# Blockwise causal attention and a maxout layer on one core: all of the layer's weights loaded ahead of two groups of q and k

## The chip, the core, the metric

The kernel runs on one core of a Trainium2 chip. The metric is device time in microseconds (us) from start to end of the program. An engine is named as the profile names it: PE (TensorE, matmuls), PEld (its weight loads), DVE (VectorE), ACT (ScalarE), POOL (GpSimd), SP (SyncE, which here only issues transfers). Each runs its own list of instructions strictly in the order written, and waits for others by semaphores.

## What is computed

Eight batches of eight heads, 576 tokens, head dimension 64, all float32 in and out. Attention is causal by blocks of 64 tokens; its output is laid out as 4608 tokens by 512 and goes through a two-branch layer.

```python
scores = scale * np.matmul(q, k.transpose(0, 1, 3, 2))
mask = block_i >= block_j                  # blocks of 64
attn = softmax(np.where(mask, scores, -1e9))
x = (attn @ v).transpose(0, 2, 1, 3).reshape(4608, 512)
g = np.maximum(x @ w1, x @ w2)             # 512 x 1024 each
out = g @ w_out                            # 1024 x 512
```

## The kernel before

**Algebra.** max(x w1, x w2) is x w2 + relu(x (w1 - w2)). So the kernel forms D = w1 - w2 (`diff_w`, line 183, four column pieces on DVE), M = w2 w_out (`m_unit`, line 249, on PE, after `bT_unit`, line 238, has transposed w2), and then out = relu(x D) w_out + x M. `h_unit(i, f)` (line 226) is one of eight 128-column pieces of relu(x D) for a span i of 512 tokens: four matmuls of 512 columns and an eviction on DVE (line 231). `y_unit` (line 268) is one 128-token tile of the output: four matmuls with M, eight with w_out.

**Attention.** The 64 heads are 32 pairs, two pairs a group, 16 groups; a batch is two groups. For a group, q and k are loaded in float32 (`load_qk`, line 115, on SP's queue), cast to bfloat16 (`cast`, line 155, mostly on POOL), transposed on PE (`transposes`, line 357) and copied out by DVE and ACT (line 365). `pad_keys` (line 383, POOL) makes a padded copy of some key columns. The scores of a pair go through `tile_0`, `tile_1`, `tile_2` (lines 376 and 394) into one of two PSUM buffers; `exp` (line 400, ACT) empties it, with a small corner exp at line 458; `mask` (line 405, POOL) zeroes four corners. `av` (line 486, PE) multiplies with v, and `x_out` transposes the result into xT on PE (lines 524 and 526, copied at 529 and 530; from group 8 on by DMA). `done_tokens` then says how many tokens the layer may work on. The first two groups (pairs 0 to 3) use finer pieces, `burst_*`.

**Order.** The order is written out by hand up to group 2 and by a loop from group 3 on. Between the attention steps, `fill(n)` issues the next ready units of the list bT, M, h, y: n counts 512-column matmuls (an M matmul counts half, a bT transpose a quarter). In the loop `fill_of(g)` sets how much is filled beside group g: the ready work less `KEEP`, shared over the groups left to the next batch boundary. `av_with(p - LAG, lo)` places av two pairs behind the scores.

**Transfers.** w2, w_out, w1 and v are issued by POOL (lines 180, 189, 177, 159) and share one software queue; q, k and the output are issued by SP. A load of q or k with `gated=True` is held back by a POOL memset of one column of its buffer (line 114): SP can issue it only after POOL has come to that place in its list. v(b, c) is piece c of five of batch b's values.

Before, the last part of the hand order runs thus on POOL: masks of pairs 2 and 3, w1(0), gates of group 2, masks, w1(1), w1(2), masks, w1(3), cast of q of group 2, gates of group 3, cast of k, v of batch 1.

Of the kernel before, what the change touches and what calls it, by code (L numbers as in the profile page):

```python
# [10 lines left out]
AF = mybir.ActivationFunctionType  # L11
# [3 lines left out]
def kernel(  # L15
# [10 lines left out]
    nc = tc.nc  # L26
# [4 lines left out]
    HP = H // 2  # L31
# [75 lines left out]
    def load_qk(g, queues, gated=False):  # L107
        b, u = divmod(g, GPB)
        for nm, src, queue in (("q", q, queues[0]), ("k", k, queues[1])):
            if queue is None or by_dma(nm, g):  # L110
                continue
            raws[nm, g] = t = raw.tile([P, 2, RPP * D], FP32, name=f"{nm}raw")
            if gated:
                nc.gpsimd.memset(t[:, 0, :1], 0.0)
            queue.dma_start(
                out=t[:],
                in_=src[b, 4 * u:4 * u + 4].rearrange(
                    "(s h) (p t) d -> (h p) s (t d)", h=2, t=RPP),
            )
# [4 lines left out]
    def by_dma(nm, g):  # L124
        return g >= T_DMA.get(nm, NG)

    def load_blocks(nm, g):
        b, u = divmod(g, GPB)
        blk_n[nm, g] = n = raw.tile([P, S // BLK, 2, D], BF16, name=f"{nm}b", tag=f"{nm}raw")
        for h in range(2):  # L130
            for s in range(2):
                nc.gpsimd.dma_start(  # L132
                    out=n[h * BLK:(h + 1) * BLK, :, s],
                    in_=(q if nm == "q" else k)[b, 4 * u + 2 * s + h].rearrange(
                        "(j p) d -> p j d", p=BLK),
                )
# [10 lines left out]
    def cast(nm, g, parts):  # L147
        if by_dma(nm, g):
            return
        t = raws[nm, g].rearrange("p s (t d) -> p t s d", d=D)  # L150
        if (nm, g) not in qk_n:
            qk_n[nm, g] = qkn.tile([P, RPP, 2, D], BF16, name=f"{nm}n")
        n = qk_n[nm, g]
        for copy, j0, j1 in parts:
            copy(out=n[:, j0:j1], in_=t[:, j0:j1])  # L155

    def load_v(b, c):
        rows = min(P, S - c * P)
        nc.gpsimd.dma_start(  # L159
            out=vv_r[b % NV][P - rows:, c, :, :D],  # L160
            in_=v[b, :, c * P:c * P + rows, :].rearrange("h p d -> p h d"),
        )
# [12 lines left out]
    def load_w1(j):  # L175
        w1_raw[j] = wraw.tile([P, NDM, WB], FP32, name="w1raw")
        nc.gpsimd.dma_start(out=w1_raw[j][:], in_=w1r[:, :, j * WB:(j + 1) * WB])
# [41 lines left out]
    def h_unit(i, f):  # L219
        if f == 0:  # L220
            g_tiles[i] = g_pool.tile([P, NFF, SPAN], BF16, name="g")
        g = g_tiles[i]
        t0 = i * SPAN
        pt = ps_m.tile([P, SPAN], FP32, name="ps_h", tag="m")
        for c in range(NDM):
            nc.tensor.matmul(  # L226
                pt[:], d_sb[:, c, f * P:(f + 1) * P], xT[:, c, t0:t0 + SPAN],
                start=(c == 0), stop=(c == NDM - 1),
            )
            if c == NDM - 1:  # L230
                nc.vector.tensor_scalar_max(g[:, f], pt[:], 0.0)  # L231
            yield

    def bT_unit(j):
# [89 lines left out]
    def ready():  # L324
        return int(sum(n * cost for n, _, need, cost in current + todo if need <= done_tokens[0]))
# [73 lines left out]
    def exp(p, ps, w, a0):  # L399
        nc.scalar.activation(  # L400
            out=aT_r[p % NA][:, :, a0:a0 + w], in_=ps[:, :, :w], func=AF.Exp, scale=scale,
        )

    def mask(p, a0, eng=None):
        (eng or nc.gpsimd).memset(aT_r[p % NA][BLK:, :, a0:a0 + BLK], 0.0)  # L405
# [27 lines left out]
    def masks_q(p, eng=None):  # L433
        for a in (1024, 1408):
            mask(p, a, eng)
# [3 lines left out]
    def tile_0(p):  # L439
        u = ps_s.tile([P, 2, 512], FP32, name="ps_s", tag="s")  # L440
        scores(p, u, 0, 0, 0, 512)
        return lambda: (exp(p, u, 512, 0), mask(p, 0))

    def tile_1(p):
        u = ps_s.tile([P, 2, 512], FP32, name="ps_s", tag="s")
        scores(p, u, 0, 0, 512, 64)
        scores(p, u, 64, 1, 128, 448)
        return lambda: (exp(p, u, 512, 512), mask(p, 576))

    def tile_2(p):  # L450
        u = ps_s.tile([P, 2, 512], FP32, name="ps_s", tag="s")
        corner_scores(p, u, 320)
        scores(p, u, 0, 2, 256, 320)
        scores(p, u, 384, 3, 448, P)

        def out():
            exp(p, u, 512, 1024)
            nc.scalar.activation(  # L458
                out=aT_r[p % NA][BLK:, :, 1536:AW], in_=u[BLK:, :, 320:320 + BLK],
                func=AF.Exp, scale=scale,  # L460
            )
            mask(p, 1024)
            mask(p, 1344)
        return out

    def region(*tiles):
        for out in tiles:
            out()

    def av(p, ts):  # L470
        b, hp = divmod(p, HP)
# [69 lines left out]
    def fill_of(g):  # L541
        if g == NG - 1:
            return 45
        left = 5 - g if g < 5 else 2 - (g - 5) % 2
        return -(-max(0, ready() - KEEP) // left)


    def pool_work(s):
        g, i = divmod(s, 2)
        if s == 4:  # L550
            load_qk(4, (SP, SP), gated=True)
        elif s == 5:
            load_qk(5, (SP, SP), gated=True)
            cast("q", 4, ((pool, 0, RPP),))
            cast("k", 4, ((pool, 0, RPP),))
        else:
            if i == 1 and g + 3 < NG:
                load_qk(g + 3, (SP, SP), gated=True)
            if i == 1 and g + 2 < NG:
                cast("q", g + 2, ((pool, 0, RPP),))  # L560
                cast("k", g + 2, ((pool, 0, RPP),))
            nb, j = divmod(s + 2, HP)
            if nb < B:
                for c in ((0, 1), (2, 3), (4,), ())[j]:
                    load_v(nb, c)
            for nm in "qk":
                if i == 1 and g + 3 < NG and by_dma(nm, g + 3):
                    load_blocks(nm, g + 3)

    T_AT = {s: [("qk"[s % 2], s // 2 + 1)] for s in range(NPAIR - 2)}  # L570
    T_AT[0] = T_AT[1] = T_AT[2] = T_AT[3] = []
# [51 lines left out]
    masks_p(2)  # L623
    masks_p(3)
    load_w1(0)
    load_qk(2, (SP, SP), gated=True)
    fill(2)
    av(1, [2, 3, 4])
    burst_q1(2)
# [13 lines left out]
    av(2, [2, 3, 4])  # L643
    burst_q3(3)
    masks_q(3)
    load_w1(3)
    cast("q", 2, ((pool, 0, RPP),))
    load_qk(3, (SP, SP), gated=True)
    cast("k", 2, ((pool, 0, RPP),))
    load_v(1, 0)  # L650
    fill(8)
    av(3, [2, 3, 4])
    fill(4)
    x_out(1, 0, NCH, (act, act))
    fill(4)
    transposes("q", 2, (dve, act))()
    transposes("k", 2, (dve, act))()
    pad_keys(4)
    pad_keys(5)
    load_v(1, 1)  # L660
    diff_w(0)
    fill(4)
    region(tile_0(4), tile_1(4))
    load_v(1, 2)
    load_v(1, 3)
    fill(8)
    region(tile_2(4), tile_0(5))
    load_v(1, 4)
    diff_w(1)
    fill(8)  # L670
    region(tile_1(5), tile_2(5))
    diff_w(2)
    cast("q", 3, ((pool, 0, RPP),))
    cast("k", 3, ((pool, 0, RPP),))
    fill(4)
    diff_w(3)
    n = fill_of(GPB)
    fill(n // 2)
    transposes("q", 3, (dve, act))()
    pool_work(4)  # L680
    fill(n // 3)
    transposes("k", 3, (dve, act))()
    pad_keys(6)
    pad_keys(7)
    pool_work(5)
    fill(n - n // 2 - n // 3)

    for g in range(GPB + 1, NG):
        a, b = 2 * g, 2 * g + 1
        old = done_tokens[0]  # L690
        if x_due:
            x_out(x_due.pop())
        n, new = fill_of(g), done_tokens[0]
        region(tile_0(a), tile_1(a))
        lo, hi = max(3, n // 18), n * 2 // 9
        for p, tiles in ((a, lambda: (tile_2(a), tile_0(b))), (b, lambda: (tile_1(b), tile_2(b)))):
            done_tokens[0] = old if p == a and x_by_dma(g - 2) else new
            fill(hi)
            av_with(p - LAG, lo)
            done_tokens[0] = new  # L700
            if p % 2 and x_by_dma(g - 1):
                x_dma(g - 1)
            if p % 2 == 0:
                for nm in "qk":
                    if g + 1 < NG and by_dma(nm, g + 1):
                        transpose_blocks(nm, g + 1)
            copy_out = t_pair(p)
            outs = tiles()
            copy_out()
            region(*outs)  # L710
            if p % 2 and g + 1 < NG:
                pad_keys(p + 1)
                pad_keys(p + 2)
            pool_work(p)
        x_due.append(g - 1)
        fill(n - 2 * (lo + hi))
    for p in range(NPAIR - LAG, NPAIR):
        if x_due:
            x_out(x_due.pop())
        av_with(p, 5)  # L720
        if p % 2 and x_by_dma(p // 2):
            x_dma(p // 2)
        fill(9)
# [42 lines left out]
```

## Time and profile before

| | |
|---|---|
| median of 4 runs | 258.94 us (257.89 to 260.35) |
| profiled execution | 258.81 us, its span 257.0 us |
| granted TensorE clock, mean | 0.997 |
| PE busy | 245.9 us, 96% |
| DVE, ACT, POOL busy | 149.9, 119.5, 122.9 us |
| HBM read, written | 34.60, 9.44 MB |
| w1 pieces, issue to landing (median) | 14.9 us |
| first scores of pair 6 (group 3) | 45.36 us |

The span runs from the first to the last instruction; the program's time is 1.8 us longer. All places below are us from the start of the span. Matmuls are pipelined: the record of a 512-column matmul lasts 0.38, but 36 of them follow each other in 7.77, 0.216 each. In a row of the timeline the bracket says how long the engine stood idle before it and what released it. In the waits a row reads: who waited, for whom, us in total, times, longest. In the DMA answers an issue line gives KB each and us from issue to landing, a queue line packets, MB and the time its packets took as a share of 16 engines; q0 is POOL's software queue, q1 SP's.

### The profile page before, as it was taken

What the parts mean: (1) busy time and instruction counts of PE and PEld (TensorE: products, weight loads), DVE (VectorE), ACT (ScalarE), POOL (GpSimd) and SP (SyncE); (2) the same over time, 40 slices, a digit from 0 to 9 for tenths busy, and PEclk for the clock granted to TensorE, in tenths of its full rate; (3) what the DMA queues carried; (4) which work ended last, traced back from release to release, by engine and by line L of the source; (5) the groups of instructions that cost most, each with busy time, mean ns of one, the idle gap of its engine ahead of it and who ended that gap; (6) DMA issues with size and microseconds to landing.
All of it is one profiled execution on the core that took longest, in us unless ns stands there. A gap on an engine that the chain in (4) does not pass through costs nothing.

```text
span 257.0 us, 6746 instructions
## 1 busy us (share of the span) xinstructions
PE 245.9 (96%) x2768; PEld 132.7 (52%) x2768; DVE 149.9 (58%) x300; ACT 119.5 (47%) x159; POOL 122.9 (48%) x289
## 2 busy tenths in 40 slices
PE   8897998989899999999999999999999999999994
PEld 2465753546455555555555555555545564444443
DVE  4986669656576447645754575457535754753521
ACT  2776394687665555555555546464646400000000
POOL 1984475579868456845685568557331100000000
PEclk9999999999999999999999999999999999999998
DMA  7999999979999999999999999999961312101122
GB/s 250 206 160 246 345 311 73 360 55 220 186 169 214 155 219 145 216 158 211 152 210 158 212 154 205 162 214 160 117 127 60 92 42 82 43 35 49 68 95 83
DMA packets 104383, 41.27 MB, mean 161 GB/s; under 512 B 89248, under 2 KB 93728, under 8 KB 104352
## 3 DMA queue, kind: packets, MB, share of 16 engines
q0 software_dynamic: 65952, 11.87, 59.9%
q1 hardware_dynamic: 37984, 28.32, 46.7%
q10 hardware_dynamic: 416, 0.66, 0.7%
q8 instruction: 21, 0.34, 0.6%
q14 instruction: 10, 0.08, 0.2%
HBM read 34.60 MB, written 9.44 MB: 171 GB/s over the span
## 4 chain that ended last, share of the span: by engine, by line
PE 82%; ACT 6%; DMA 5%; POOL 3%; issue 2%; SPq 0%; DVE 0%; POOLq 0%; ACTq 0%
PE ps_y L268 35%; PE ps_h L226 22%; PE ps_o L486 10%; PE ps_s L376 7%; ACT aT L400 4%; DMA kraw<-in_k_dram 4%; PE ps_w L346 2%; PE ps_qT L357 2%; DMA qraw<-in_q_dram 2%; POOL qn L155 1%; PE ps_y L283 1%; POOL kn L155 1%; ACT kT L365 1%; PE ps_s L411 1%; PE ps_s L394 1%
## 5 line engine op out<-in xcount | busy, mean ns | idle before, releaser
L400 ACT ACTIVATE aT<-ps_s 128x1024 bf16<-128x1024 f32 (+2 forms) x100 | 95.8, 994 | 43.7 <-PE ps_s L376 32.7
L268 PE MATMUL ps_y<-wo_sb,g 128*128 128x512 bf16 x280 | 71.2, 380 | 0.0
L226 PE MATMUL ps_h<-xT,d_sb 128*128 128x512 bf16 x288 | 67.9, 380 | 0.0
L231 DVE TENSOR_SCALAR g<-ps_h 128x512 bf16<-128x512 f32 x72 | 49.6, 690 | 18.4 <-PE ps_h L226 18.3
L405 POOL MEMSET aT<- 64x128 bf16 x128 | 23.1, 201 | 66.0 <-ACT aT L400 65.2
L273 DVE COPY y<-ps_y 128x512 f32<-128x512 f32 x35 | 24.2, 692 | 45.5 <-PE ps_y L268 44.7
L486 PEld LDWEIGHTS <-aT 128*128 128x128 bf16 x960 | 37.4, 98 | 14.0 <-issue 0.5
L226 PEld LDWEIGHTS <-d_sb 128*128 128x128 bf16 x288 | 26.5, 98 | 31.3 <-issue 2.5
L268 PEld LDWEIGHTS <-g 128*128 128x128 bf16 x280 | 24.7, 98 | 30.3 <-issue 5.7
L486 PE MATMUL ps_o<-vv,aT 128*128 128x65 bf16 x960 | 39.8, 194 | 0.0
L268 PE MATMUL ps_y<-m_sb,xT 128*128 128x512 bf16 x140 | 38.4, 380 | 0.0
L159 POOL DMA_DIRECT2D vv<-in_v_dram x40 | 33.9, 854 | 1.0 <-issue 0.5
L376 PE MATMUL ps_s<-qT,kT 64*128 64x128 bf16 (+6 forms) x344 | 31.6, 281 | 2.6 <-ACT aT L458 1.5
L493 DVE TENSOR_TENSOR xp<-ps_o,rec 128x256 bf16<-128x256 f32 (+1 forms) x64 | 31.4, 491 | 2.2
L132 POOL DMA_DIRECT2D kb<-in_k_dram x40 | 29.4, 759 | 0.0
L492 DVE RECIPROCAL rec<-ps_o 128x4 f32<-128x4 f32 (+1 forms) x64 | 12.0, 187 | 23.2 <-PE ps_o L486 22.9
L288 ACT COPY y<-ps_y 128x256 f32<-128x256 f32 (+1 forms) x2 | 0.6, 319 | 49.3 <-PE ps_y L283 49.3
L365 ACT COPY qT<-ps_qT 128x576 bf16<-128x576 bf16 x15 | 9.6, 639 | 26.6 <-PE ps_qT L357 26.6
L155 POOL CAST qn<-qraw 128x1152 bf16<-128x1152 f32 (+1 forms) x15 | 17.3, 1154 | 7.5 <-DMA qraw<-in_q_dram 7.4
L268 PEld LDWEIGHTS <-xT 128*128 128x128 bf16 x140 | 12.8, 98 | 13.5 <-issue 0.5
L376 PEld LDWEIGHTS <-kT 64*128 64x128 bf16 x344 | 11.9, 94 | 14.2 <-issue 9.0
L365 DVE COPY qT<-ps_qT 128x576 bf16<-128x576 bf16 x17 | 12.8, 750 | 0.9 <-PE ps_qT L357 0.9
(58 smaller groups left out, 135.9 us busy)
## 6 DMA issues: line engine op xcount, KB each, us to landing
qraw<-in_q_dram SPq DMA_DIRECT2D x16, 576.0 KB, 4.8
out_dram<-y SPq DMA_DIRECT2D x35, 256.0 KB, 3.9
vv<-in_v_dram POOLq DMA_DIRECT2D x32, 128.0 KB, 5.6
kraw<-in_k_dram SPq DMA_DIRECT2D x5, 576.0 KB, 7.5
kb<-in_k_dram POOLq DMA_DIRECT2D x40, 72.0 KB, 6.2
w1raw<-in_moe_w_dram POOLq DMA_DIRECT2D x4, 512.0 KB, 14.9
xT<-in_moe_w_dram POOLq DMA_DIRECT2D x4, 256.0 KB, 6.9
wo_sb<-in_moe_w_out_dram POOLq DMA_DIRECT2D x2, 512.0 KB, 11.9
```

The lines of the kernel that those rows point to most:

```text
L132: nc.gpsimd.dma_start(out=n[h * BLK:(h + 1) * BLK, :, s], in_=(q if nm == "q" else k)[b, 4 * u + 2 * s + h].rearrange("(j p) d -> p j d", ...
L159: nc.gpsimd.dma_start(out=vv_r[b % NV][P - rows:, c, :, :D], in_=v[b, :, c * P:c * P + rows, :].rearrange("h p d -> p h d"),)
L226: nc.tensor.matmul(pt[:], d_sb[:, c, f * P:(f + 1) * P], xT[:, c, t0:t0 + SPAN], start=(c == 0), stop=(c == NDM - 1),)
L231: nc.vector.tensor_scalar_max(g[:, f], pt[:], 0.0)
L268: nc.tensor.matmul(py[:], lhs, rhs, start=(n == 0), stop=(n == len(terms) - 1),)
L273: nc.vector.tensor_copy(out=y[:], in_=py[:])
L365: (copy or copies[i])(out=t[:, p0 * RPP:p1 * RPP].rearrange("q (p j) -> q p j", j=RPP), in_=pts[i][:, :, p0:p1].rearrange("q j p -> q p j"),)
L376: nc.tensor.matmul(ps[:, hh, col:col + w], kT[r, k0:k0 + P], qT[r, q0:q0 + w], start=True, stop=True,)
L400: nc.scalar.activation(out=aT_r[p % NA][:, :, a0:a0 + w], in_=ps[:, :, :w], func=AF.Exp, scale=scale,)
L405: (eng or nc.gpsimd).memset(aT_r[p % NA][BLK:, :, a0:a0 + BLK], 0.0)
L486: nc.tensor.matmul(po[:, gi, hh, :], a[:, hh, a0:a0 + P], vv[:, c, h0 + 2 * hh, :], start=(mm == 0), stop=(mm == n_mm - 1),)
L493: nc.vector.tensor_mul(xp[:, :, ts[0]:ts[0] + n, p % 2].rearrange("q s t d -> q t s d"), po[:, :, :, :D], rec[:, :n].to_broadcast([P, n, 2 ...
```

## The change

It reorders the hand-written part and the start of the loop; no unit of work is added or taken away.

- Loads: q and k of group 2 are gated after w1(0) to w1(2) and before w1(3), group 3 right after w1(3), instead of after w1(0) and after the cast of q. v of batch 1 follows at once, its pieces 0 and 1 ahead of the casts.
- The last five M units run in one piece (part of `fill(4)`, and `fill(16)`) ahead of the transposes of group 2, which stood among them; three of the four `diff_w` come before these transposes; one h unit stands between q's and k's.
- The first two h units are evicted by ACT (relu) instead of DVE.
- Masks of pairs 4 and 5 come in one piece later on POOL (`masked=False`, `masks(p)`), and group 3's transposes stand among the scores of pair 5. Gates and casts of groups 4 and 5 move with them, out of `pool_work`.
- In the loop, av(6) runs at the end of group 3 and av(7) in the slot of pair 8; pair 9's slot takes `x_out(3)`. `KEEP` is 0 up to group 4.

```diff
             if c == NDM - 1:
-                nc.vector.tensor_scalar_max(g[:, f], pt[:], 0.0)
+                if i == 0 and f < 2:
+                    nc.scalar.activation(out=g[:, f], in_=pt[:], func=AF.Relu)
+                else:
+                    nc.vector.tensor_scalar_max(g[:, f], pt[:], 0.0)
             yield
...
+    def masks(p):
+        for a0 in (0, 576, 1024, 1344):
+            mask(p, a0)
+
-    def region(*tiles):
+    def region(*tiles, masked=True):
         for out in tiles:
-            out()
+            out(masked)
...
-        return -(-max(0, ready() - KEEP) // left)
+        return -(-max(0, ready() - (KEEP if g > GPB + 2 else 0)) // left)
...
     masks_p(3)
     load_w1(0)
-    load_qk(2, (SP, SP), gated=True)
     fill(2)
...
     masks_q(3)
+    load_qk(2, (SP, SP), gated=True)
     load_w1(3)
+    load_qk(3, (SP, SP), gated=True)
+    load_v(1, 0)
+    load_v(1, 1)
     cast("q", 2, ((pool, 0, RPP),))
-    load_qk(3, (SP, SP), gated=True)
+    load_v(1, 2)
     cast("k", 2, ((pool, 0, RPP),))
-    load_v(1, 0)
+    load_v(1, 3)
+    load_v(1, 4)
     fill(8)
     av(3, [2, 3, 4])
     fill(4)
     x_out(1, 0, NCH, (act, act))
     fill(4)
+    diff_w(0)
+    diff_w(1)
+    diff_w(2)
+    fill(16)
     transposes("q", 2, (dve, act))()
+    fill(4)
     transposes("k", 2, (dve, act))()
     pad_keys(4)
     pad_keys(5)
-    load_v(1, 1)
-    diff_w(0)
-    fill(4)
-    region(tile_0(4), tile_1(4))
-    load_v(1, 2)
-    load_v(1, 3)
-    fill(8)
-    region(tile_2(4), tile_0(5))
-    load_v(1, 4)
-    diff_w(1)
-    fill(8)
-    region(tile_1(5), tile_2(5))
-    diff_w(2)
+    diff_w(3)
     cast("q", 3, ((pool, 0, RPP),))
+    load_qk(4, (SP, SP), gated=True)
     cast("k", 3, ((pool, 0, RPP),))
     fill(4)
-    diff_w(3)
-    n = fill_of(GPB)
-    fill(n // 2)
-    transposes("q", 3, (dve, act))()
-    pool_work(4)
-    fill(n // 3)
+    region(tile_0(4), tile_1(4), masked=False)
+    fill(8)
+    region(tile_2(4), tile_0(5), masked=False)
+    masks(4)
+    fill(8)
+    copy_out = transposes("q", 3, (dve, act))
+    outs = tile_1(5), tile_2(5)
+    copy_out()
+    region(*outs, masked=False)
+    fill(4)
     transposes("k", 3, (dve, act))()
     pad_keys(6)
     pad_keys(7)
-    pool_work(5)
-    fill(n - n // 2 - n // 3)
+    masks(5)
+    load_qk(5, (SP, SP), gated=True)
+    cast("q", 4, ((pool, 0, RPP),))
+    cast("k", 4, ((pool, 0, RPP),))
+    fill(4)
...
             fill(hi)
-            av_with(p - LAG, lo)
+            if p == 9:
+                x_out(3)
+                new = done_tokens[0]
+            else:
+                av_with(p - 1 if p == 8 else p - LAG, lo)
...
-        x_due.append(g - 1)
+        if g != GPB + 2:
+            x_due.append(g - 1)
         fill(n - 2 * (lo + hi))
+        if g == GPB + 1:
+            av_with(6, lo)
```

More of the change, by code (lines that the diff above doesn't have):

```diff
@@ L441, in tile_0 @@
         scores(p, u, 0, 0, 0, 512)
-        return lambda: (exp(p, u, 512, 0), mask(p, 0))
+        return lambda masked: (exp(p, u, 512, 0), masked and mask(p, 0))
     def tile_1(p):
@@ L447, in tile_1 @@
         scores(p, u, 64, 1, 128, 448)
-        return lambda: (exp(p, u, 512, 512), mask(p, 576))
+        return lambda masked: (exp(p, u, 512, 512), masked and mask(p, 576))
     def tile_2(p):
@@ L454, in tile_2, with out @@
         scores(p, u, 384, 3, 448, P)
-        def out():
+        def out(masked):
             exp(p, u, 512, 1024)
@@ L461, in out @@
             )
-            mask(p, 1024)
-            mask(p, 1344)
-        return out
-    def region(*tiles):
+            if masked:
+                mask(p, 1024)
+                mask(p, 1344)
+        return out
+    def masks(p):
+        for a0 in (0, 576, 1024, 1344):
+            mask(p, a0)
+    def region(*tiles, masked=True):
         for out in tiles:
-            out()
+            out(masked)
     def av(p, ts):
@@ L544, in fill_of @@
         left = 5 - g if g < 5 else 2 - (g - 5) % 2
-        return -(-max(0, ready() - KEEP) // left)
+        return -(-max(0, ready() - (KEEP if g > GPB + 2 else 0)) // left)
     def pool_work(s):
         g, i = divmod(s, 2)
[L550 to L568, printed above, removed]
+        if i == 1 and g + 3 < NG:
+            load_qk(g + 3, (SP, SP), gated=True)
+        if i == 1 and g + 2 < NG:
+            cast("q", g + 2, ((pool, 0, RPP),))
+            cast("k", g + 2, ((pool, 0, RPP),))
+        nb, j = divmod(s + 2, HP)
+        if nb < B:
+            for c in ((0, 1), (2, 3), (4,), ())[j]:
+                load_v(nb, c)
+        for nm in "qk":
+            if i == 1 and g + 3 < NG and by_dma(nm, g + 3):
+                load_blocks(nm, g + 3)
     T_AT = {s: [("qk"[s % 2], s // 2 + 1)] for s in range(NPAIR - 2)}
```

## The prediction

> **What bounds the kernel now.** I read the page first, then stretches of time, then TensorE's waits, then the DMA answers of the stretch that the change touches. TensorE (PE) is full from 70 us to the end of the matmuls, so the time is PE's fixed work plus the holes in its first 70 us.
>
> ```profile
> PE   8897998989899999999999999999999999999994
> PEclk9999999999999999999999999999999999999998
> ```
>
> The stretches give the holes in us (first number the length, second PE busy; the 1.00 after the engines is the granted clock):
>
> ```profile
> 23.40:45.36 21.96, 18.59 (x234) 11.51 (x235) 14.67 (x23) 11.74 (x20) 12.74 (x26) 1.00 1.27 250
> 45.36:70.00 24.64, 23.07 (x398) 13.59 (x399) 14.32 (x34) 17.53 (x23) 20.04 (x45) 1.00 1.09 204
> 70.00:253.00 183.00, 183.00 (x1825) 95.84 (x1824) 102.74 (x201) 74.51 (x97) 75.21 (x182) 1.00 1.05 140
> ...
> 255.50:256.00 0.50, 0.00 (x0) 0.00 (x0) 0.00 (x0) 0.00 (x0) 0.00 (x0) 0.68 0.00 0
> ```
>
> 21.96 - 18.59 = 3.37 us are idle between 23.40 (last scores of pair 3) and 45.36 (first scores of pair 6), 24.64 - 23.07 = 1.57 up to 70, none after. PE's waits from 20 to 70 us name them:
>
> ```profile
> PE ps_M L249 <- DMA wo_sb<-in_moe_w_out_dram: 1.6, 1, 1.6
> PE ps_s L376 <- ACT aT L458: 1.5, 2, 0.8
> PE ps_qT L357 <- POOL qn L155: 1.0, 1, 1.0
> PE ps_kT L357 <- POOL kn L155: 0.5, 1, 0.5
> ```
>
> The first, third and fourth are landings, or casts behind landings; the second is exponentials that hold a score buffer. The whole prize is 3.37 + 1.57 = 4.9 us: no change of order can make this kernel faster than about 253.9.
>
> How long loads take is in the DMA answers, for single issues: w_out's first half, q and k of group 2 (issued 19.19 and 19.60), q and k of group 3 (27.70 and 28.18):
>
> ```profile
> wo_sb<-in_moe_w_out_dram POOLq DMA_DIRECT2D x1, 512.0 KB, 10.6
> qraw<-in_q_dram SPq DMA_DIRECT2D x1, 576.0 KB, 7.2
> kraw<-in_k_dram SPq DMA_DIRECT2D x1, 576.0 KB, 9.9
> qraw<-in_q_dram SPq DMA_DIRECT2D x1, 576.0 KB, 9.6
> kraw<-in_k_dram SPq DMA_DIRECT2D x1, 576.0 KB, 12.5
> ```
>
> And who shares the engines, in three stretches: 19.6 to 22.4, 23 to 27, 32 to 34 us (packets, MB):
>
> ```profile
> q0 software_dynamic: 1096, 0.55, 145.3%
> ```
>
> ```profile
> q1 hardware_dynamic: 447, 0.99, 72.5%
> q0 software_dynamic: 481, 0.25, 44.6%
> ```
>
> ```profile
> q0 software_dynamic: 121, 0.45, 61.5%
> q1 hardware_dynamic: 122, 0.28, 42.0%
> ```
>
> Until 22.4 nothing of group 2 moves, though q was issued at 19.19. Then q, k take 0.99 of 1.24 MB from w_out (small packets), but against w1 (3.7 KB a packet to their 2.3) they get 0.28 of 0.73. Packet counts are about equal in both: the queues take turns by packet.
>
> **The change, part by part.** Times are of the profiled execution: span 257.0, 258.81 in all, 0.13 below the median of the four runs (258.94).
>
> 1. w_out alone. From 22.4 to 25.03 its queue crept at 0.25 MB / 4 us = 62 KB/us instead of 0.55 / 2.8 = 196. With q, k gone, the 0.14 MB moved from 22.8 to 25.0 take 0.7 us: landing at 23.5 at best, 25.03 at worst. I take 24.0, as a straggling engine rather than the mean lands last: PE waits 0.6 from 23.40 instead of 1.63.
>
> 2. M in one piece. In before, two units, an av, a unit (25.03 to 28.50) are 3.47, x_out 0.41, the next unit 0.98. Units 5 to 8 are 32 matmuls at 1.86/16 = 0.116: 3.7. Sum 8.56, so M ends at 24.0 + 8.56 = 32.6. Its evictions go to ACT, idle then. w_out's second half landed 29.7 before; it is needed at 28.9 now, with less ahead of it: nothing.
>
> 3. q, k of group 2 issued later. Their gates pass POOL's masks, w1(1) and w1(2): after the last mask (23.99 + 0.20) the gate is at 24.23, and by the 0.13 from gate to issue SP starts q at 24.36, k at 24.77. SP has nothing else queued. With q's first bytes 3.2 to 3.6 us after issue they meet w1, not w_out. Bounds for k: 9.9 and 12.5 after issue, 34.7 to 37.3. The w1 neighbourhood is that of group 3, though fewer straggling bytes are ahead: I take 11.6, so 36.4; for q 9.0 (of 7.2 to 9.6), 33.4. From landing to the first transpose before: k landed 29.5, the cast ran 1.14, transposes began 30.84, so 1.32.
> PE stands from 32.6 to 34.7 (33.4 + 1.32): 2.1. Then 0.37 of q transposes and one h unit, 0.97: 36.05. k's transposes start at 36.4 + 1.32 = 37.7: 1.65 more. v(1,2) now sits between the casts (0.89 on POOL), done by 35.6, before k lands: nothing. v(1,0) and v(1,1), 0.89 each, run while POOL waits anyway, and their packets queue behind w1. While POOL waits for k, v(1,3), v(1,4) and the pads stand behind it: v(1,4) is issued near 39.5 instead of 37.79 and at its 8.3 lands near 47.8; its av is not before 49, so that costs nothing, with 1.2 to spare.
>
> 4. diff_w ahead of the q copies. Three at 1.23 on DVE, idle there; free unless w1(2) lands after 34.7 (36.6 before; with q, k out of its way I expect 33). Then DVE, in order, holds qT and all behind it.
>
> 5. Relu on ACT for two h units. A 128x256 cast there is 0.37, a 128x1024 exp 1.02, so about 0.6 each; the second stands before the first exp, and one score tile waits 0.15. DVE is spared 2 x 0.69.
>
> 6. Masks, pads, gates for groups 4 and 5, casts: the same instructions. The 4 masks of pair 4 now follow k's cast of group 3 but are needed at its av, some 10 us later; 4 x 0.20 is nothing.
>
> 7. Groups 3 and 4. The 0.82 wait ahead of group 4 goes: av(6), 0.91, and six more y matmuls, 1.3, now lie in it. In group 4 the slot of pair 9 has x_out instead of an av, so ACT leads. ACT before, in that group:
>
> ```profile
> 59.04 0.64 ACT L365 COPY qT<-ps_qT 128x576 bf16<-128x576 bf16 x1 [1.50 <-PE ps_qT L357]
> 59.58 1.03 ACT L400 ACTIVATE aT<-ps_s 128x1024 bf16<-128x1024 f32 x1
> 60.63 0.27 ACT L458 ACTIVATE aT<-ps_s 64x128 bf16<-64x128 f32 x1
> 60.93 1.02 ACT L400 ACTIVATE aT<-ps_s 128x1024 bf16<-128x1024 f32 x1
> ```
>
> From the end of q's transposes (58.85) ACT needs 3.1 to 61.95, then 0.6 copy, 1.95 for two exps, 0.27: 5.9. PE's work up to the second score tile of group 5 was 65.24 - 0.69 - 58.85 = 5.7; less the av (0.91) and one y (0.22): 4.6. So 1.3 idle, where before had 0.69. Net of both: 1.3 - 1.51 = -0.2; bounds -1.5 (ACT ahead by then) and +0.6.
>
> 8. KEEP and the new fill counts move matmuls between slots and add none; PE is full from 70 us on, which hides it. If a slot starved, its units would be missing from the row at 70.
>
> Sum: 0.6 + 2.1 + 1.65 + 0.15 = 4.5 against 3.37, +1.1; step 7, -0.2; +0.9. The other way round: from k's transposes to pair 6 the rows add to 9.2, so 46.9, where before stood at 45.36 with one h unit (0.87) still to do, 46.23: +0.7, less 0.2, +0.5. I take +0.8: **259.6**.
>
> Two rules weigh on this. The Trainium skill, "DMA: Bandwidth & Descriptors", Latency and other measured facts, gives a hardware queue about 0.6 us to its first byte. The trace disagrees under load (nothing from 19.56 to 22.4). By the rule q, k would start about 2.7 us earlier, k land near 34, and the sum be near 257.
>
> The second speaks against the rival below. The skill's "TensorE: Matmul & The Clock Gate", Part 1, says the clock halves after an idle window of about 3.4 us; no wait here is that long, so by it the clock stays and the sum too. The row above gives 0.68 in 255.50 to 256.00, hence a drop at 255.7, only 2.2 us after the last matmul at 253.44.
>
> **The rivals.**
>
> The clock drops (slower). Waits of 2.1 and 1.65 with 1.3 of work between them are near the 2.2 after which it fell; 1.63, the longest wait of before, left it at 1.00. It decides if the wait for q passes some 2.2. Price: 16 warm-up matmuls took 6.21 at the start where 16 x 0.216 = 3.46 would do, so 2.75 at most; the wait for k hides up to 1.65 of it, leaving 1.1 to 2.75, I say 1.8: 261.4.
>
> The loads come as fast as group 2's did (7.2 and 9.9). For: fewer bytes ahead. Against: w1 in large packets. k at 34.7 takes 1.7 from the waits: 257.9; with ACT's new wait gone too, 256.4.
>
> The queue of group 3 slips: its casts were waited for 0.98 in before, one of them ran 1.96 instead of 1.14, and its loads now follow group 2's at once. Against: it is needed 6 and 8 us after k's transposes. About +2: 261.6.
>
> The reordering is hidden anyway, landings and all: 258.8; it is inside the main case's range.
>
> **How the numbers follow.** Main case 0.48, own range 258.2 to 260.8; fast loads 0.24 (255.8 to 258.2); clock 0.18 (260.8 to 262.6); group 3 late 0.10. What this kernel's measurement can tell is about 1%, 2.6 us: under 256.35 is faster, over 261.53 slower. Faster: half of the fast loads, 0.12. Slower: half of the clock case, 0.09, most of the late one, 0.07, a little of the main, 0.02: 0.18. Same: 0.70. The range leaves out the outer tenth on each side: 256.5 to 261.8.
>
> **What would show it.** PE's wait for w_out near 0.6; q and k of group 2 landing near 33.4 and 36.4; PE waits of about 2 and 1.6 us on the two casts; the first scores of pair 6 near 47; a wait of some 1.3 on the exps in group 4; clock 1.00 throughout. k before 35 or a clock under 1.00 would make it wrong.

## The result and the profile after

| | before | after |
|---|---|---|
| median | 258.93 us (64 runs, 257.37 to 264.98) | 260.05 us (43 runs, 258.94 to 262.06) |
| profiled execution, its span | 258.81, 257.0 | 259.87, 258.1 |
| granted TensorE clock, mean | 0.997 | 0.993 |
| first scores of pair 6 | 46.23 (45.36 and the h unit that came later) | 47.98 |

The ratio of after to before is 1.0047, 95% interval [1.0031, 1.0063]: 0.5% slower, less than the 1% that the prediction held this measurement able to tell, but with an interval that excludes 1. Runs over 1.5% above the fastest of the same kernel are left out of the ratios and of the groups by clock below, not of the medians in the tables; of those timed with the experiments all but one, of 631 us, had a mean clock of 0.985 to 0.993.

The page's first hint is one digit: PE's and the clock's share of the span, in 40 slices.

```profile
PE   8897959999899999999999999999999999999994
PEclk9999988999999999999999999999999999999999
```

The two 8s in the clock, missing before, lie at and behind the 5 in PE: TensorE waited, and then ran slower. The stretches of after, with the same columns as before (length, then PE busy; after the engines, clock):

```profile
23.40:45.36 21.96, 18.01 (x212) 11.29 (x212) 11.71 (x18) 9.93 (x17) 11.99 (x24) 0.92 1.32 278
45.36:70.00 24.64, 23.73 (x371) 13.17 (x367) 14.44 (x33) 19.49 (x27) 17.32 (x44) 1.00 0.97 161
70.00:254.00 184.00, 184.00 (x1879) 97.10 (x1877) 103.96 (x205) 75.57 (x98) 78.72 (x187) 1.00 1.08 142
```

Here 3.95 us are idle in the first stretch (3.37 before) and its clock is 0.92; 0.91 in the second (1.57 before); none later. PE's waits from 20 to 73 us (who, for whom, us, times, longest):

```profile
PE ps_qT L360 <- POOL qn L155: 2.4, 1, 2.4
PE ps_M L252 <- DMA wo_sb<-in_moe_w_out_dram: 1.3, 1, 1.3
PE ps_kT L360 <- POOL kn L155: 0.6, 1, 0.6
PE ps_kT L360 <- DVE xT L537: 0.4, 1, 0.4
PE ps_s L379 <- ACT aT L461: 0.3, 1, 0.3
```

The same in PE's timeline (start, duration, instructions, wait in brackets):

```profile
24.41 1.92 PE L252 MATMUL ps_M<-wo_sb,bT_sb 128*128 128x256 bf16 x16 [1.27 <-DMA wo_sb<-in_moe_w_out_dram]
...
28.29 4.54 PE L252 MATMUL ps_M<-wo_sb,bT_sb 128*128 128x256 bf16 x40
35.21 0.44 PE L360 MATMUL ps_qT<-ident,qn 64*128 64x64 bf16 x18 [2.38 <-POOL qn L155]
35.58 1.04 PE L226 MATMUL ps_h<-xT,d_sb 128*128 128x512 bf16 x4
37.18 0.66 PE L360 MATMUL ps_kT<-ident,kn 64*128 64x64 bf16 x18 [0.56 <-POOL kn L155]
37.77 1.89 PE L226 MATMUL ps_h<-xT,d_sb 128*128 128x512 bf16 x4
```

The same four matmuls of an h unit take 1.04 at 35.58 and 1.89 at 37.77. Where the clock lies, the stretches show:

```profile
33.25:36.67 3.42, 1.41 (x22) 0.63 (x22) 1.15 (x2) 0.65 (x2) 2.66 (x3) 1.00 1.21 338
36.67:40.08 3.41, 2.90 (x28) 1.15 (x28) 1.89 (x2) 1.60 (x3) 3.26 (x5) 0.50 1.97 206
```

In 3.42 us of mostly waiting PE is busy for 1.41; the next 3.41 are at half clock. And the landings, for single issues in stretches that hold only one, q and k of group 2:

```profile
qraw<-in_q_dram SPq DMA_DIRECT2D x1, 576.0 KB, 9.7
kraw<-in_k_dram SPq DMA_DIRECT2D x1, 576.0 KB, 11.1
```

Issued at 24.12 and 24.53, they landed at 33.8 and 35.6. In the rows of POOL the casts follow:

```profile
34.01 1.14 POOL L155 CAST qn<-qraw 128x1152 bf16<-128x1152 f32 x1 [7.18 <-DMA qraw<-in_q_dram]
35.10 0.88 POOL L159 DMA_DIRECT2D vv<-in_v_dram  x1
35.97 1.16 POOL L155 CAST kn<-kraw 128x1152 bf16<-128x1152 f32 x1
```

Who shares the engines, from q's issue to its first bytes (24.12 to 27.9 us), and from there to 34 us (packets, MB, share):

```profile
q0 software_dynamic: 628, 1.33, 114.4%
```

```profile
q1 hardware_dynamic: 529, 1.17, 56.3%
q0 software_dynamic: 526, 0.96, 50.6%
```

Nothing of q moves for 3.8 us. Then the packets are equal in number, as before, and q and k get 1.17 of 2.13 MB.

In group 4, ACT's rows answer to those shown of before:

```profile
63.00 0.64 ACT L368 COPY qT<-ps_qT 128x576 bf16<-128x576 bf16 x1 [1.21 <-PE ps_s L397]
63.54 1.03 ACT L403 ACTIVATE aT<-ps_s 128x1024 bf16<-128x1024 f32 x1
...
66.36 1.95 ACT L403 ACTIVATE aT<-ps_s 128x1024 bf16<-128x1024 f32 x2
68.33 0.27 ACT L461 ACTIVATE aT<-ps_s 64x128 bf16<-64x128 f32 x1
```

From the first copy on ACT has no pause until the corner exp at 68.33, whose end releases PE's scores at 68.66.

The ledger, up to pair 6: the three waits are 1.27 + 2.38 + 0.56 = 4.21, against 3.37 idle before: +0.84. PE came to the first of them 0.25 earlier (23.15 for 23.40). Pair 6 is 47.98 - 46.23 = 1.75 late, so 1.75 - 0.84 + 0.25 = 1.16 are left for the clock. Behind it: 0.44 + 0.33 = 0.77 of waits for 0.82 + 0.69 = 1.51, -0.74. 1.75 - 0.74 = +1.0; the spans differ by 1.03.

### The profile page after: what moved, and what is told of

Read it like the earlier page. It is cut to its first block, busy times and chain, and to the rows that moved or that the text cites. A ratio compares the mean times of both kernels' runs of the same rounds, so it can differ in the third digit from the quotient of the medians.

```text
span 258.1 us, 6752 instructions
## 1 busy us (share of the span) xinstructions
PE 246.8 (96%) x2768; PEld 133.3 (52%) x2768; DVE 148.5 (58%) x298; ACT 121.0 (47%) x161; POOL 122.9 (48%) x289
## 4 chain that ended last, share of the span: by engine, by line
PE 88%; ACT 4%; DMA 4%; POOL 1%; issue 1%; DVE 1%; POOLq 0%; ACTq 0%
PE ps_y L271 35%; PE ps_h L226 24%; PE ps_o L494 11%; PE ps_s L379 9%; DMA qraw<-in_q_dram 4%; ACT aT L403 3%; PE ps_w L349 2%; PE ps_qT L360 2%; PE ps_y L286 1%; PE ps_s L414 1%; PE ps_s L397 1%; PE ps_bT L241 1%; PE ps_kT L360 1%; POOL kn L155 0%; POOL qn L155 0%
## 5 line engine op out<-in xcount | busy, mean ns | idle before, releaser
L226 PE MATMUL ps_h<-xT,d_sb 128*128 128x512 bf16 x288 | 69.1, 383 | 0.0
L234 DVE TENSOR_SCALAR g<-ps_h 128x512 bf16<-128x512 f32 x70 | 48.3, 691 | 18.6 <-PE ps_h L226 18.6
L155 POOL CAST qn<-qraw 128x1152 bf16<-128x1152 f32 (+1 forms) x15 | 16.5, 1100 | 11.7 <-DMA qraw<-in_q_dram 11.7
L379 PEld LDWEIGHTS <-kT 64*128 64x128 bf16 x344 | 11.9, 95 | 13.4 <-issue 7.8
```

What stands on the lines that cost most here:

```text
L226: nc.tensor.matmul(pt[:], d_sb[:, c, f * P:(f + 1) * P], xT[:, c, t0:t0 + SPAN], start=(c == 0), stop=(c == NDM - 1),)
L379: nc.tensor.matmul(ps[:, hh, col:col + w], kT[r, k0:k0 + P], qT[r, q0:q0 + w], start=True, stop=True,)
```

## The experiments

Theory A is this ledger: after loses about 0.8 in the waits for q and k and 1.2 in clock, and gains 0.7 in the loop. Its rivals (B): the clock drop is harmless, since engines other than PE pace groups 2 and 3 and would take back what is saved; and the loads alone, or the order on PE alone, make the difference. Each kernel was timed beside the kernel before. "Full clock" below means a mean clock of 0.997 or more: before's 0.997 comes from one drop at 255.7 us, behind its last matmul.

| kernel | median (range), us | ratio to before |
|---|---|---|
| e1_busy_wait | 258.97 (258.27 to 260.42) | 1.0000 [0.9966, 1.0034] |
| e2_h_first | 258.30 (257.80 to 259.81) | 0.9979 [0.9947, 1.0011] |
| e3_loads_alone | 267.05 (266.74 to 267.29) | 1.0292 [1.0247, 1.0337] |
| e4_loads_back | 259.65 (258.46 to 262.22) | 1.0018 [0.9981, 1.0054] |
| e5_loop_alone | 258.29 (256.79 to 261.24) | 0.9967 [0.9929, 1.0005] |
| e6_loop_casts | 257.80 (256.59 to 262.20) | 0.9957 [0.9922, 0.9992] |
| e7_h_first_v | 257.98 (257.54 to 259.92) | 0.9967 [0.9933, 1.0001] |
| e8_before_busy | 258.80 (257.98 to 264.30) | 0.9997 [0.9966, 1.0027] |
| e9_casts_busy | 257.45 (256.94 to 631.26) | 0.9951 [0.9925, 0.9976] |
| e10_casts_busy_2 | 258.00 (257.09 to 258.75) | 0.9969 [0.9938, 1.0001] |

**e1_busy_wait: the wait for q filled with work that nobody needs.** Nine matmuls on zeros; their result goes nowhere.

```diff
     fill(16)
+    warm_up(9)
     transposes("q", 2, (dve, act))()
```

> The changed kernel with nine 512-column matmuls on zeros (1.94 us at full clock) set into PE's 2.38 us wait for the cast of q of group 2; their result goes nowhere. Theory A (the drop of the clock, 3.41 us at half, is part of the price): the clock stays at 1.00, nothing else moves, and PE does in that stretch what took it 1.4 us more: 260.05 - 1.4 = 258.6, ratio to before 0.999. Theory B (from the landing of k on the exponentials pace PE, so a slow PE there costs nothing): the clock stays, but the holes come back as waits for exps in groups 2 to 4; 259.7 to 260.1, ratio 1.004. If the clock drops all the same, idleness is not what drops it.

Measured: 258.97, 1.1 below after and 0.4 above what A expected. Ten of its twelve runs had the full clock, as none of after's had; the other two took 260.42 and 260.25. In PE's timeline the transposes stand where they did in after, and the clock doesn't fall:

```profile
35.22 0.44 PE L360 MATMUL ps_qT<-ident,qn 64*128 64x64 bf16 x18 [1.43 <-POOL qn L155]
35.59 1.04 PE L226 MATMUL ps_h<-xT,d_sb 128*128 128x512 bf16 x4
37.19 0.44 PE L360 MATMUL ps_kT<-ident,kn 64*128 64x64 bf16 x18 [0.56 <-POOL kn L155]
37.56 1.04 PE L226 MATMUL ps_h<-xT,d_sb 128*128 128x512 bf16 x3
...
43.33 0.44 PE L360 MATMUL ps_qT<-ident,qn 64*128 64x64 bf16 x18
```

q's transposes are at 35.22 (35.21 in after), k's at 37.19 (37.18), yet those of group 3 stand at 43.33 instead of 44.59: 1.26 us with nothing changed but the clock. They are still there at group 5 (70.88 for 72.15) and in the span (256.9 for 258.1). In this execution M ended at 31.85, so without the zeros nearly nothing would have been busy from 31.90 to 35.31, the clock's period there (see the last section). A's clock term is shown, and it isn't given back; that part of B falls.

**e2_h_first: useful work in the wait.** Two h units are brought forward into it.

```diff
-    fill(16)
+    fill(24)
     transposes("q", 2, (dve, act))()
```

> The changed kernel with two h units (eight matmuls, 1.73 us) taken from later slots and put into the wait for q. A: the wait shrinks from 2.38 to 0.65, the clock stays: 260.05 - 1.7 - 1.4 = 256.9, ratio 0.992. B: the wait shrinks and the clock stays, but the two units are missing later, as waits for exps in groups 2 to 4: 258.6 to 259.5, ratio 0.999 to 1.002.

Measured: 258.30. In the profile the clock stays at 1.00 (in eight of the twelve runs it is full), but 1.73 us of work moved forward bring only 0.4 more than e1 (70.51 for 70.88 at group 5). PE's waits say where the rest is; three of these rows are new or longer than in after:

```profile
PE ps_s L379 <- ACT aT L461: 0.7, 1, 0.7
...
PE ps_s L379 <- DVE kT L368: 0.6, 1, 0.6
PE ps_kT L360 <- POOL kn L155: 0.6, 1, 0.6
PE ps_kT L360 <- DVE xT L537: 0.6, 1, 0.6
```

The scores now wait 0.6 for the copy of kT, and ACT's exponential holds them 0.7 in group 4 instead of 0.3. With the clock out of the way, k's landing, the copies and the exponentials hold PE up in groups 2 to 4: by these waits B is right for this part.

**e3_loads_alone: before, with the loads' new places only.**

```diff
     load_w1(0)
-    load_qk(2, (SP, SP), gated=True)
...
+    load_qk(2, (SP, SP), gated=True)
     load_w1(3)
+    load_qk(3, (SP, SP), gated=True)
+    load_v(1, 0)
+    load_v(1, 1)
     cast("q", 2, ((pool, 0, RPP),))
-    load_qk(3, (SP, SP), gated=True)
+    load_v(1, 2)
     cast("k", 2, ((pool, 0, RPP),))
```

(v(1,3) and v(1,4) follow, and go from their later places.)

> The kernel before with the loads of the changed kernel alone (POOL's order of w1, gates and v), PE's order as before. A (the late landings of q and k are the loss, and M in one piece and the rest of the new order win some of it back): q's transposes stand ready near 29.3 and wait to about 35, the clock drops, k's at 37.2; from there to pair 6 before needed 13.5, so some 5 us later: 264, ratio 1.02. The rival (the new order of the loads costs little, the rest of the change is the loss): 259 to 260.

Measured: 267.05, three us more than expected. The stretches show a long wait and the clock low for three periods, in the first of them with no work at all:

```profile
27.44:30.86 3.42, 1.37 (x26) 0.97 (x26) 0.85 (x2) 1.18 (x2) 0.00 (x0) 1.00 1.04 361
30.86:34.27 3.41, 0.00 (x0) 0.00 (x0) 0.00 (x0) 0.00 (x0) 0.00 (x0) 0.50 1.13 342
34.27:37.69 3.42, 0.66 (x18) 0.50 (x18) 0.76 (x1) 0.64 (x1) 2.75 (x3) 0.50 1.26 330
37.69:41.10 3.41, 2.99 (x32) 1.83 (x32) 2.22 (x3) 1.01 (x2) 3.26 (x5) 0.50 2.03 150
```

In before's order four M units, 3.7 us of work, stand behind q's transposes, and PE waits 7.3 us for q; after has these units ahead and waits 2.38. That M in one piece is what makes the late loads bearable is argued from this; no run adds it alone to e3.

**e4_loads_back: after, with the loads of groups 2 and 3 where before had them** (`diff_w` 1 to 3 follow the landings of w1, as they must with w1 late again).

```diff
     load_w1(0)
+    load_qk(2, (SP, SP), gated=True)
     fill(2)
...
-    diff_w(1)
-    diff_w(2)
     fill(16)
```

> The changed kernel with group 2's and 3's loads where they were before (after w1(0), and after the cast of q), and the second to fourth diff_w set where their w1 lands then; M in one piece and the rest as changed. A: the waits for q and k (2.38 and 0.56) and the clock's drop go, the wait for w_out grows from 1.27 to 1.63, one h unit waits for its D near 34.3; 257.0 to 257.6, ratio 0.993. The rival (the rest of the change is the loss): 260, ratio 1.004.

Measured: 259.65, two us more than A expected and near the rival's 260; its interval takes in 1, so it is resolved neither from before nor from after. The waits for q and k are gone, and others stand in their place:

```profile
PE ps_h L226 <- DVE d_sb L183: 3.4, 3, 1.8
PE ps_M L252 <- DMA wo_sb<-in_moe_w_out_dram: 1.2, 2, 0.6
```

With M used up early, the h units come when D isn't there: 3.4 us of waits for w1 and the `diff_w` behind it, where after has 2.38 + 0.56 = 2.94 for q and k. In the second row 0.65 is a wait for w_out's second half. So setting the loads back takes away one wait and brings another of its size: in both orders the work that needs none of w1, q and k runs out there. That a third order couldn't do better isn't shown.

**e5_loop_alone: before, with the loop's part only** (`KEEP`, av(6), av(7), x_out(3)).

```diff
-        return -(-max(0, ready() - KEEP) // left)
+        return -(-max(0, ready() - (KEEP if g > GPB + 2 else 0)) // left)
...
-            av_with(p - LAG, lo)
+            if p == 9:
+                x_out(3)
+                new = done_tokens[0]
+            else:
+                av_with(p - 1 if p == 8 else p - LAG, lo)
...
+        if g == GPB + 1:
+            av_with(6, lo)
```

> The kernel before with the loop's part of the change alone: av(6) at the end of group 3, av(7) in pair 8's slot, x_out(3) in pair 9's, KEEP 0 up to group 4. A (this part gains what step 7 of the prediction says, and more, since the changed kernel's profile has 0.77 of waits there against 1.51): the 0.82 wait ahead of group 4 goes, ACT's wait in group 4 stays near 0.7 in sum; 0.7 less than before, 258.1, ratio 0.997. The rival (the freed time comes back as waits on ACT): same as before, 258.8.

Measured: 258.29, 0.7 under the 258.97 beside it; the interval [0.9929, 1.0005] just takes in 1, so by itself this gain isn't resolved. Among runs with the full clock it is 257.51 (6) for 258.31 (18 of before), -0.8. A's term is met, and the waits in groups 3 and 4 are those of after. Its profiled execution shows the clock once more:

```profile
27.58:30.99 3.41, 1.35 (x27) 0.95 (x26) 1.17 (x3) 1.82 (x3) 1.26 (x4) 1.00 1.06 366
30.99:34.41 3.42, 3.05 (x32) 1.82 (x32) 2.28 (x3) 1.01 (x2) 2.60 (x4) 0.50 1.04 358
```

**e6_loop_casts: e5, with the casts of group 3 earlier** and pair 4's and 5's masks in one piece behind them, so that the 0.98 wait for a cast of group 3 goes.

```diff
-    region(tile_2(4), tile_0(5))
+    region(tile_2(4), tile_0(5), masked=False)
+    masks(4)
     load_v(1, 4)
+    cast("q", 3, ((pool, 0, RPP),))
+    load_qk(4, (SP, SP), gated=True)
     diff_w(1)
```

> The kernel before, its loads and M as they were, with the loop's part and the later masks: group 3's casts no longer stand on POOL behind the masks of pair 5 (and so behind its exps), and the gate of group 4 comes before the cast of k. A: the 0.98 wait for q of group 3 goes as well, 258.8 - 0.7 - 1.0 = 257.1, ratio 0.993, below both kernels. The rival (q of group 3 lands too late for it, or the time returns in groups 3 and 4 as waits on ACT): as the loop alone, 258.1.

Measured: 257.80, 0.7 above what was expected, ratio 0.9957 [0.9922, 0.9992]: faster than both kernels. What it has over e5 isn't resolved; with the full clock both have 257.5. Its profiled execution was one of the long ones, 261.76 us: w_out's first half landed 13.4 us after its issue, M started at 27.83, PE was busy for 0.70 us in the clock's period ahead of 28.53, and the next period was at half clock.

**e7_h_first_v: e2, with v(1,2) behind the cast of k.** In after, the cast of k stood 0.37 behind its landing (35.97 for 35.6), since POOL was issuing v(1,2).

```diff
-    load_v(1, 2)
     cast("k", 2, ((pool, 0, RPP),))
+    load_v(1, 2)
     load_v(1, 3)
...
-    fill(16)
+    fill(24)
```

> The changed kernel with two h units in the wait for q, as in the run above, and v(1,2) behind the cast of k instead of ahead of it. k landed 35.6 and its cast began 35.97, behind that issue. A: k's transposes start 0.34 earlier and with them all that ACT paces: 258.3 - 0.3 = 258.0, ratio 0.997. The rival (the cast was late for another reason): 258.3, no change.

Measured: 257.98, as expected, 0.3 under e2, but not resolved from it. In its profile k's cast waited 0.82 for the landing itself, so this execution can't show the gain. Inconclusive.

**e8_before_busy and e9_casts_busy: matmuls on zeros in the wait for w_out**, in before and in e6.

```diff
+    warm_up(6)
     fill(8)
     av(3, [2, 3, 4])
```

> The kernel before, with 6 matmuls on zeros, whose result goes nowhere, ahead of M's first unit, where TensorE waits 1.63 us for w_out: 6 x 0.216 = 1.3 us of work in that wait. In the runs of before so far, 39 of 53 had a mean clock of 0.997 or more and medians of 258.3 to 258.4; 14 had 0.991 to 0.993 and medians of 260.4 to 260.7. Theory C: the time of before varies with the clock, and the clock with the wait for w_out; then nearly all runs here are at 0.997 or more, the median is near 258.4, the ratio to before some 0.998, and times over 260 are rare. Theory D: a late landing makes both, the lower clock and most of the 2 us; then the clock is full, but about a quarter of the runs still take 260 us or more and the median stays at before's. If the landing is early, the 1.3 us stand in the way and the time is up to 1 us longer.

> The kernel of e6_loop_casts (the kernel before with the change's loop part and the casts of group 3 earlier), with the same 6 matmuls on zeros ahead of M's first unit. It has the same wait for w_out, and 9 of its 10 runs had the full clock already, at a median of 257.53. Theory C: full clock in nearly all runs, 257.4 to 257.7, ratio 0.994 to 0.996. Theory D: as e6_loop_casts, 257.8 with a few runs near 259. If the zeros delay M whenever w_out is early: 258.0 to 258.8.

Measured: e8 258.80, no gain. Ten of its twelve runs had the full clock, with a median of 258.67; before's full-clock runs beside it have 258.69. But there the kernel before had the full clock in 19 of 23 runs as it was, for 48 of the 75 beside the other experiments, so there was little for the zeros to win. Nor do they always keep the clock: the two others, at 0.993 and 0.992, took 262.79 and 264.30, and in e8's profile w_out comes so late (PE starts M at 26.23, for 25.03 in before) that PE still waits 1.62 behind the zeros. A third run took 260.26 at full clock. Neither C nor D is met in full, and how much of before's spread is clock and how much landing stays open.

e9 took 257.45, the lowest median here, 0.9951 [0.9925, 0.9976]. One of its executions, the profiled one, took 631 us: a 512-column matmul's record lasted 825 ns instead of 380 from beginning to end. So the kernel was run again.

**e10_casts_busy_2: e9 unchanged.**

> The kernel of e9_casts_busy once more, because the execution profiled there took 631 us and its trace can't be set beside the others. If that was one execution's trouble: 257.2 to 257.7, ratio 0.994 to 0.997, all clocks at 0.997 or more; in the profile no wait for the casts of q and k of group 3, a wait of under 0.5 us for w_out or none behind the zeros, and the waits in groups 3 and 4 of e5_loop_alone (0.4 for DVE's copy of x_out(3), 0.3 for an exponential). If the zeros themselves bring on such executions, another of 600 us or so is among its 12.

Measured: 258.00, 0.3 above the expected range, 0.9969 [0.9938, 1.0001]; full clock in all twelve runs, nothing near 631. The only waits of 0.3 us or more:

```profile
PE ps_kT L357 <- POOL kn L155: 1.4, 1, 1.4
PE ps_kT L357 <- DVE xT L534: 0.4, 1, 0.4
PE ps_s L376 <- ACT aT L458: 0.3, 1, 0.3
```

The waits for w_out and for group 3 are gone, as expected; that for k of group 2 is left. Without the run of 631 us the 23 of e9 and e10 have a median of 257.7. So the kernel before gains with the change's loop part and the later masks and casts (e6), or with these and zeros in the wait for w_out (e9), while its loads and M stay where they were.

## Why the prediction came out near the time, by its own steps

The forecast was 259.6, the median is 260.05, within the main case's range and on the side it named. But that was partly luck, since two errors cancel in it: up to pair 6 it lost more than forecast, and behind it gained more. And by a sign that it had named itself, "a clock under 1.00 would make it wrong", the main case's mechanism failed.

1. **w_out alone (0.6).** 1.27. Half of w_out landed 10.0 us after its issue, for 10.6 before, where the step's 24.0 took some 9.6. One trace can't price this: in the five traces with q and k loaded later (after, e1, e2, e3, e7) it took 9.0 to 10.0, in the six with them in front (before, e4, e5, e6, e8, e10) 8.8 to 13.4. The landing varies by more between executions than the step was worth. The three over 10.0 are all among the six, which fits the step's reason, but with one execution each it isn't shown.

2. **M in one piece.** Held: 24.41 + 8.56 = 32.97; the wait for q began at 35.21 - 2.38 = 32.83. So did "nothing" for w_out's second half, with "less ahead of it": it landed 9.3 to 10.5 us after its issue in the five traces, 12.3 to 14.0 in the six, and in e4 PE waited 0.65 for it.

3. **q, k later (2.1 and 1.65).** q held: landed 33.8 for 33.4, wait 2.38. k failed in size: 0.56. It landed at 35.6, 11.1 after its issue for the 11.6 taken, and the issue was 0.24 earlier (24.53 for 24.77). q's later transposes had also used up part of its wait. "v(1,2): nothing" was wrong by up to 0.37, the delay of k's cast. q's first bytes came at 27.9, 3.8 after the issue, for the 3.2 to 3.6 taken from before's trace. The rule of the Trainium skill weighed there ("DMA: Bandwidth & Descriptors", Latency and other measured facts: about 0.6 us to the first byte of a hardware queue) isn't met here either.

4. and 5. **`diff_w`, relu on ACT.** No wait of PE names either; the third `diff_w` began at 32.41, when its w1 piece had landed, ahead of q's transposes.

6. **Masks, casts, group 3.** Held, and the rival "group 3 late" fell. Its q and k took 12.3 and 13.6 us to land, and PE waited for neither.

7. **Groups 3 and 4 (-0.2).** -0.7. ACT's rows held: 5.9 were forecast from the end of q's transposes to the scores of group 5's second tile; the timeline has 62.88 to 68.66, 5.8. What failed is PE's work beside it, put at 4.6. PE waited 0.33 + 0.44 = 0.77 instead of 1.3, so its work was about 5.0. More than half of that wait was not for ACT at all, but for DVE's copy of x_out(3), which the step hadn't priced.

8. **KEEP.** Held: no hole behind 70 us.

**The clock.** The step that failed is: "no wait here is that long, so by it the clock stays and the sum too". The prediction kept this apart as a rival with 0.18, decided "if the wait for q passes some 2.2"; it was 2.38. The price, put at 1.8 between 1.1 and 2.75, was 1.26 by e1. The error lay in judging by the longest wait. The forecast's own waits, 2.1 and 1.65 with 1.34 of work between them, leave at most 1.3 busy in any 3.41 us that hold the first wait whole; in after 1.41 were busy in the period ahead of the drop.

Without the clock's 1.26 the loss up to pair 6 would have been 1.75 - 1.26 = 0.5 (forecast: 1.1), and with the loop's -0.7 the whole about -0.2: no change, as e1 shows (1.0000).

The rival "fast loads" fell: q came 9.7 and k 11.1 after issue, not 7.2 and 9.9. "The reordering is hidden" fell with e3 and e5: its parts are worth +8 and -0.7.

## What to carry to other kernels

- Where a move opens a wait on TensorE, count what is busy in the 3.4 us around it, not the length of the longest wait. Here the new waits cost 0.84 more than the old ones and the clock 1.26 on top, and nine matmuls on zeros won the latter back.
- A load moved behind another pays only if there is work that needs neither. In after and in e4 the work ran out, and about 3 us of waiting went from q and k to w1 or back.
- Split a change before judging it: this one held a gain of 0.7 us in the loop and a loss of 1.8 in its first half.

## What the runs showed of the hardware

**The clock is decided by the busy share of a fixed period.** Drops and returns lie a multiple of 3.41 us apart in every trace that has them. In the profiled executions of before, after and e1 to e8 and e10, no such period between 20 and 70 us with PE busy for 1.93 us or more was followed by half clock. Those with 1.41 or less were, each time: after (1.41), e5 (1.35), e3 (1.37, 0.00, 0.66), e6 (0.70). The nearest on the safe side are e1's and before's:

```profile
31.90:35.31 3.41, 1.93 (x14) 0.77 (x15) 1.03 (x1) 0.36 (x1) 1.29 (x2) 1.00 1.18 339
```

```profile
23.58:26.99 3.41, 1.96 (x23) 1.78 (x24) 0.88 (x3) 0.35 (x1) 1.57 (x4) 1.00 1.17 314
```

So the bound lies between 41% and 57% busy. The end of e4 narrows it: its last matmuls kept PE busy for 1.51 us between 252.87 and 256.28, 44% of that period, and the clock stayed at 1.00 behind them; in before 1.15 us between 252.27 and 255.68 were followed by half clock. The periods don't start with the program: a boundary is at 33.25 in after, at 31.90 in e1, so the same wait can fall into one period or be shared by two. The Trainium skill, "TensorE: Matmul & The Clock Gate", Part 1, gives the free-running period of 3413 ns, which agrees; but it speaks of an idle window, and of no gap over 3.4 us, and here a 2.38 us gap was enough.

**A program on one core has several times, and the mean clock tells them apart.** Of the 86 runs of before that count beside the experiments, 67 had a mean clock of 0.997 or more, with a median of 258.43; 19 had 0.990 to 0.993, with 260.47. Of 44 executions of after none had the full clock: 33 had one period less (0.992 to 0.993, 259.88), 11 two (0.984 to 0.987, 261.06). In after a further period costs 1.2 us. The 2.0 in before are more than that; a late landing may make the rest, as in e6's long execution, but no run divides the two.
